# Weights laid out by pairs of units in DRAM: loads and whole-row stores of 6,144 bytes per partition behind attention

## The chip, the cores and the metric

One core of a Trainium2 chip runs the kernel in one launch. The metric is device time in microseconds, the median of several executions; lower is better. Before the change it is 380.92 us (three runs: 380.85, 380.92, 381.82).

## The reference

Sigmoid attention feeds a soft mixture of experts. All tensors are float32.

```python
# attention: B, H, S, D = 8, 12, 448, 64
scores = scale * q @ k.transpose(0, 1, 3, 2) - log(S)
attn_out = (1 / (1 + exp(-scores))) @ v
x = attn_out.transpose(0, 2, 1, 3).reshape(B * S, H * D)      # 3584 x 768
# soft MoE: 8 experts with 4 slots each, w1[e] 768 x 1024, w2[e] 1024 x 768
logits = x @ phi                                              # 3584 x 32
d = softmax(logits, axis=0)
slot_input = (d.T @ x).reshape(8, 4, 768)
for e in range(8):
    slot_out[e] = relu(slot_input[e] @ w1[e]) @ w2[e]
c = softmax(logits, axis=1)
return c @ slot_out.reshape(32, 768)                          # 3584 x 768
```

The weights w1 and w2 are 25.2 MB each and the output is 11.0 MB.

## The kernel before

The program has two parts in a row. **Attention** goes through 168 units `u = (p, c)` (pair of heads, block of 128 keys) in a software pipeline. Per step PE makes the scores of one unit (L188), ScalarE the sigmoid (L196), and PE weighs the values of the unit two steps before (L229). Between these stand the DVE transposes, the logits and the slot sums of the batch before. After the last unit, `last_job` finishes the last batch's logits, softmax and slot inputs, about 278 to 289 us.

**Behind attention** the experts are computed. The weights come in 128 *units* of [128, 768] floats (384 KB, 3,072 bytes per partition): 64 of w1 (expert, half of the rows, quarter of the columns), then 64 of w2 (half of the output columns `hf`, expert, `g`, `y`). `w1_part(e)` takes eight units in two groups of four; `w2_step(n)` takes two units, `y` 0 and 1, of one `(hf, e, g)`. The first column half is computed for all experts (sixteen steps, with the combine softmax turned into lhsT tiles `cts` between them), then the second half (sixteen steps). `spread_sum` sums each half's four partial sums into the tile `sts[hf]`. The output is `cts.T @ sts[hf]` in tiles of 128 tokens by 384 columns, which ScalarE and VectorE copy out of PSUM in turn (L579). `out_half(m, hf)` stores two such blocks of tokens in one half of the columns (runs of 1,536 bytes in DRAM), `out_rows(m)` one block in whole rows (runs of 3,072 bytes). Nine `out_half` for the first half stand among the steps 4 to 12 of the second half; after the second `spread_sum` come ten `out_rows` (blocks 18 to 27) and nine `out_half` for the second half.

All units, `cts` tiles and output tiles go through one ring of 71 slots of [128, 768]: 56 slots `wa` that exist from the start, two in `wpe` (which attention borrows as transposed x), and 13 slots `wb` in the memory that the attention buffers held. 58 units are loaded during attention; the 13 `wb` loads are written behind it, and the other 57 at four places of eight in the `w1_part`s.

Every transfer is issued by SyncE (SP), in the program's order, on one queue. A tile's load waits for the last readers of what lay there before. The transfers take eight semaphores in turn (`DMAHW0` to `DMAHW7`), so each waits for the transfer eight before it, and at most eight are in flight. PE, DVE, ACT and SP take their instructions in the order of the code (`manual_schedule`).

Of the kernel before, what the change touches and what calls it, by code (L numbers as in the profile page):

```python
# [9 lines left out]
F32 = mybir.dt.float32  # L10
F32R = mybir.dt.float32r
# [6 lines left out]
DM, NSLOT, E, SPE, F = 768, 32, 8, 4, 1024  # L18
P = 128
# [8 lines left out]
HALF = DM // 2  # L28
UNIT = 768
N_A = 56  # L30
N_E = 2
N_B = 13
QW = 2 * S
NP = B * NPR
WARM = 5
# [3 lines left out]
BLK = 32  # L39
NEG = -1.0e30  # L40
TR = 3
SLN = TR * 64
FW = (NFC + 1) * NSLOT
ROWS = 128
NG = B * S // ROWS
NH = 18
MANUAL = {mybir.EngineType.PE, mybir.EngineType.SP, mybir.EngineType.DVE, mybir.EngineType.Activation}


@with_exitstack  # L50
def soft_moe_attention(ctx: ExitStack, tc: tile.TileContext, qk, v, vl, phi, w1, w2, cst, out):
    nc = tc.nc
    ctx.enter_context(tc.manual_schedule(engines=MANUAL))

    cpool = ctx.enter_context(tc.tile_pool(name="cpool", bufs=1))
    small = ctx.enter_context(tc.tile_pool(name="small", bufs=1))
    wpa = ctx.enter_context(tc.tile_pool(name="wpa", bufs=1))
# [17 lines left out]

    units = [("w1", e, q, kh) for e in range(E) for kh in range(2) for q in range(4)]
    units += [("w2", hf, e, g, y) for hf in range(2) for e in range(E) for g in range(2) for y in range(2)]
    state = {"next": 0, "ring": 0, "wpb": None}
    utile = {}
    wpe = wpa.tile([P, N_E * UNIT], F32, name="wpe")  # L80

    def ring_tile(dt=F32):
        n = state["ring"] % (N_A + N_E + N_B)
        state["ring"] += 1
        if n < N_A:
            return wpa.tile([P, UNIT], dt, name=f"wa{n}")
        n -= N_A
        if n < N_E:
            return wpe[:, n * UNIT:(n + 1) * UNIT] if dt == F32 else ring_tile(dt)
        return state["wpb"].tile([P, UNIT], dt, name=f"wb{n - N_E}")  # L90

    def load_unit():
        n = state["next"]
        if n >= len(units):
            return
        state["next"] = n + 1
        u = units[n]
        t = ring_tile()[:, :]
        nc.sync.dma_start(t, w1[u[1:]] if u[0] == "w1" else w2[u[1:]])
        utile[u] = t  # L100

    heads = (slice(0, 64), slice(64, 128))
    QSCALE = 1.0 / math.sqrt(D)
# [11 lines left out]
    with ExitStack() as actx:  # L115
# [45 lines left out]
        def load_qk(p):  # L161
            if p < NP:
                t = get("qk", p % 3)
                nc.sync.dma_start(t[:], qk[p])
                qkts[p] = t
# [100 lines left out]
        def logits(lg, b, pairs, js=(3, 2, 1, 0), c0=0, c1=NBK):  # L266
            for hp in pairs:
                for j in js:
                    n = min(c1, nblk(j))
                    nc.tensor.matmul(  # L270
                        lg[32 * j:32 * j + 32, BLK * c0:BLK * n], phi_sb[:, hp, :],
                        blocks(x_of(b * NPR + hp)[:, c0 * P:], j, n - c0),
                        start=(hp == 0), stop=(hp == NPR - 1 and c1 == NBK))
# [149 lines left out]
        for r in range(NP // 2):  # L423
            p = 2 * r
# [3 lines left out]
        for b in range(B):  # L428
            u = b * per_b + LAG
# [4 lines left out]
        for b in range(B - 1):  # L434
            u = (b + 1) * per_b + LAG
# [15 lines left out]
        for i in range(len(seq) + LAG):  # L451
            for f in early.get(i, ()):
                f()
            if i < len(seq):
                u = seq[i]
                score(u)
                if u[1] == NFK:
                    load_qk(u[0] + 3)
                elif u[0] % 2 == 1 and u[1] == NFK - 1:
                    load_qk(u[0] + 3)  # L460
                while state["next"] < min(N_A, (i + 1) * N_A // W_STEPS):
                    load_unit()
                if i == (B - 1) * per_b + LAG + SLOT_AT + 1:
                    for _ in range(N_E):
                        load_unit()
            if i == len(seq) - 1:
                lgt = ps_sc.tile([P, 2, 512], F32, name="sc")
                nc.vector.memset(lgt[64:128, 0, 96:128], NEG)
            if i == len(seq):
                nc.scalar.activation(dmx[0:1, :], atts[seq[-1]][0:1, 0, 0:1], AF.Exp)  # L470
            for f in middle.get(i, ()):
                f()
            if i >= LAG:
                u = seq[i - LAG]
                weigh(u)
                p, c = u
                if i == len(seq):
                    logits(lgt[:, 0, :], B - 1, range(NPR - 1))
                if c == NFK:
                    evac_b(p)  # L480
                    load_vl(p // 2 + 1)
                elif c == NFK - 1:
                    load_v(p + 2)
                    if p == NP - 1:
                        work(B * S)
                        pw = ps_av.tile([P, 512], F32, name="av00")
                        px = [ps_av.tile([P, 512], F32, name="av01")]
                        px += [ps_sc.tile([P, 2, 512], F32, name="sc")[:, 0, :], ps_av.tile([P, 512], F32, name="av10")]
                        turn_pe(px[0], p - 1)
                        continue  # L490
                    evac_a(p)
                    if p % 2 == 1:
                        evac_b(p)
            for f in late.get(i, ()):
                f()
            work(rate.get(i, PACE))
# [12 lines left out]
        turn[name] += 1  # L509
        return ps_av.tile([P, 512], F32, name=f"{name}{turn[name] % 2}")  # L510

    for _ in range(N_B):
        load_unit()

    def w1_part(e, ph=None):
        if ph is None:
            ph = av_tile("av0")
            w1_mm(ph, e, range(TR))
        for _ in range(4):
            load_unit()  # L520
        if e == 0:
            finish(ps_t)
        w1_mm(ph, e, range(TR, NKC))
        for _ in range(4):
            load_unit()
        return ph

    def h_part(e, ph):
# [6 lines left out]
    cts = {}  # L535
# [19 lines left out]
    def combine_turn(b, c4):  # L555
        pt = ps_t.tile([P, 512], F32, name="pt")
        for c in range(NBK):
            n = P if c < 3 else 64
            c0 = c * P if b % 2 == 0 else (c * P + 64) % 448
            nc.tensor.transpose(  # L560
                out=pt[:, c0:c0 + n], in_=c4[0:n, c].rearrange("p a z s -> p (a z s)").bitcast(F32),
                identity=csb[0:n, 0:n])
        at0 = S * b
        while at0 < S * (b + 1):
            i, m = divmod(at0, UNIT)
            w = min(UNIT - m, S * (b + 1) - at0)
            if m == 0:
                cts[i] = ring_tile(F32R)
            nc.scalar.copy(cts[i][:, m:m + w], pt[:, at0 - S * b:at0 - S * b + w])
            at0 += w  # L570

    def ct_of(m):
        i, k = divmod(m * ROWS, UNIT)
        return cts[i][:, k:k + ROWS]

    def out_tile(ov, m, st, hf, n):
        pf = ps_t.tile([P, 512], F32, name="pt") if n % 2 else av_tile("av0")
        nc.tensor.matmul(pf[:, 0:HALF], ct_of(m), st, start=True, stop=True)  # L578
        (nc.scalar.copy, nc.vector.tensor_copy)[n % 2](ov, pf[:, 0:HALF])  # L579

    def out_half(m, hf):
        ov = ring_tile()[:, :].rearrange("p (j c) -> p j c", j=2)
        for j in range(2):
            out_tile(ov[:, j, :], m + j, sts[hf], hf, j)
        nc.sync.dma_start(
            out[m * ROWS:(m + 2) * ROWS, hf * HALF:(hf + 1) * HALF].rearrange("(j p) c -> p j c", p=P), ov)

    def out_rows(m):
        ov = ring_tile()[:, :].rearrange("p (j c) -> p j c", j=2)
        for hf in range(2):  # L590
            out_tile(ov[:, hf, :], m, sts[hf], hf, hf)
        nc.sync.dma_start(out[m * ROWS:(m + 1) * ROWS, :].rearrange("p (j c) -> p j c", j=2), ov)

    sts = []

# [15 lines left out]
    def w2_step(po, hf, n):  # L611
        e, g = divmod(n, 2)
        h = hw[e % 2]
        if g == 0:
            o = NSLOT - SPE
            nc.gpsimd.tensor_copy(
                h[:, o:o + NFC * NSLOT].rearrange("p (f s) -> p f s", f=NFC)[:, :, 0:SPE], hc[:, e])
        for fl in range(4):
            k = (4 * g + fl) * NSLOT + NSLOT - SPE - SPE * e
            ut = utile[("w2", hf, e, g, fl // 2)][:, fl % 2 * HALF:(fl % 2 + 1) * HALF]  # L620
            nc.tensor.matmul(  # L621
                po[32 * fl:32 * fl + 32, 0:HALF], h[:, k:k + NSLOT], ut,
                start=(n == 0), stop=(n == 2 * E - 1))
        load_unit()
        load_unit()

    prev = None
    for e in range(E):
# [17 lines left out]
    for n in range(2 * E):  # L646
        w2_step(po, 1, n)
        if n == 3:
            spread_sum(so)
        if 4 <= n < 4 + NH // 2:  # L650
            out_half(2 * (n - 4), 0)
    spread_sum(gather(po))
    for m in range(NH, NG):
        out_rows(m)
    for m in range(0, NH, 2):
        out_half(m, 1)

# [36 lines left out]
```

## Time and profile before

| What | Value |
|---|---|
| Median of three runs | 380.92 us (380.85 to 381.82) |
| Profiled execution, its own time | 379.96 us |
| Its span, first to last instruction | 378.2 us |
| Mean granted TensorE clock | 0.978 |
| PE / DVE / ACT busy in the span | 355.6 / 252.9 / 224.1 us |
| Bytes moved | 95.29 MB (83.59 MB read from HBM, 11.01 MB written) |
| Load queue | 42,336 packets, 94.62 MB, 72.3% of 16 engines' span |
| Weight loads | 128 of 384 KB |
| Output stores | 28 of 384 KB |

The span is cut by the page into 40 slices; a digit is the busy share in tenths. A share of the DMA engines may be over 1, since packets overlap on an engine. The packets of one transfer are spread over 16 engines; here a packet is one partition's row (or the part of it that is contiguous in DRAM), and each engine adds a packet of 4 bytes for the semaphore. Names such as `wa<-in_w_dram` are destination and source with buffer numbers left out: w1 and w2 both read as `in_w_dram`. L592 is the store of `out_rows`, L585 that of `out_half`, L99 a unit's load, L110 a w1 matmul, L621 a w2 matmul, L329 a matmul that adds the old slot sums in `last_job`.

### The profile page before, as it was taken

Reading aid. Unit: us, or ns where it says so; the run is one execution under the profiler, and the core shown is the slowest. Engines: PE = TensorE matmul, PEld = TensorE weight load, DVE = VectorE, ACT = ScalarE, POOL = GpSimd, SP = SyncE. Lnnn points to the kernel's source line nnn. Section 1 sums busy time; section 2 is a strip of 40 time slices with the busy share of each in tenths; the row PEclk is TensorE's granted clock in tenths of the full one; section 3 lists DMA queues with packets and bytes.
Section 4 is the critical chain, followed back from the end, with each engine's and each line's share of the span. In section 5 each row is a group of like instructions: output and inputs, shape, how many; then the busy total and the mean of one; then the engine's idle time right before and its main releaser. Section 6 shows DMA issues by size and latency. Waiting matters only on the chain.

```text
span 378.2 us, 10668 instructions
## 1 busy us (share of the span) xinstructions
PE 355.6 (94%) x4374; PEld 160.4 (42%) x4374; DVE 252.9 (67%) x681; ACT 224.1 (59%) x311; POOL 5.4 (1%) x25
## 2 busy tenths in 40 slices
PE   8999999999999999999999999999999978989750
PEld 4333444444444444444444444444456643422420
DVE  0148878885989688778859896888746872233560
ACT  4777676766757676767667675767672113422550
POOL 1000000000000000000000000000001000000000
PEclk9999999999999999999999999999999998999895
DMA  7687575766657675756666576433479999999998
GB/s 259 218 257 233 181 252 183 241 224 200 216 175 245 230 216 193 233 199 229 222 207 205 189 267 194 132 123 129 142 232 354 383 400 400 402 400 398 400 407 309
DMA packets 42384, 95.29 MB, mean 252 GB/s; under 512 B 4448, under 2 KB 18528, under 8 KB 42336
## 3 DMA queue, kind: packets, MB, share of 16 engines
q1 hardware_dynamic: 42336, 94.62, 72.3%
q8 instruction: 34, 0.56, 0.6%
q14 instruction: 14, 0.11, 0.1%
HBM read 83.59 MB, written 11.01 MB: 250 GB/s over the span
## 4 chain that ended last, share of the span: by engine, by line
PE 83%; DVE 7%; DMA 4%; ACT 1%; issue 1%; DVEq 0%; ACTq 0%
PE sc L188 34%; PE av L229 33%; PE av L621 5%; PE sc L270 3%; PE sc L323 3%; DMA wpe<-in_w_dram 2%; PE pt L560 2%; DMA out_dram<-wa 1%; DVE tmp L531 1%; DMA qk<-in_qk_dram 1%; DVE tmp L530 1%; PE av L578 1%; PE av L204 1%; DVE wa L579 1%; ACT lt L541 1%
## 5 line engine op out<-in xcount | busy, mean ns | idle before, releaser
L196 ACT ACTIVATE att<-sc,sm 128x896 f32<-128x896 f32 x167 | 168.3, 1008 | 85.1 <-PE sc L188 82.1
L188 PE MATMUL sc<-qk 64*64 64x448 f32 x1336 | 157.2, 542 | 0.5 <-DMA qk<-in_qk_dram 0.5
L229 PE MATMUL av<-att,v 64*64 64x448 f32 x1128 | 131.2, 536 | 0.0
L188 PEld LDWEIGHTS sc<-qk 64*64 64x64 f32 x1336 | 49.8, 134 | 71.5 <-issue 58.8
L254 DVE STREAM_TRANSPOSE wpe<-xy 32x256 f32<-32x256 f32 (+3 forms) x224 | 76.9, 343 | 3.7
L229 PEld LDWEIGHTS av<-att,v 64*64 64x64 f32 x1128 | 42.8, 133 | 63.2 <-issue 61.1
L254 DVE STREAM_TRANSPOSE y<-x 32x288 f32<-32x288 f32 (+1 forms) x128 | 66.5, 520 | 2.0
L236 DVE TENSOR_TENSOR x<-x,av 128x448 f32<-128x448 f32 x24 | 14.9, 621 | 31.5 <-PE av L229 24.5
L229 PE MATMUL av<-att,vl 64*64 64x448 f32 x188 | 22.3, 536 | 0.0
L236 DVE TENSOR_TENSOR xy<-xy,av 128x448 f32<-128x448 f32 x23 | 14.3, 621 | 9.8 <-ACT xy L232 4.5
L110 PE MATMUL av<-wa,jt 128*32 128x256 f32 x336 | 18.5, 380 | 0.1
L110 PEld LDWEIGHTS av<-wa,jt 128*32 128x32 f32 x336 | 10.7, 110 | 7.2 <-DVE jt L385 0.2
L621 PE MATMUL av<-wa,jt 128*32 128x384 f32 x112 | 13.4, 506 | 0.2
L578 PE MATMUL av<-lt,wb 128*128 128x384 f32 x28 | 12.5, 446 | 1.1 <-DVE lt L608 1.0
L232 ACT COPY x<-av 128x448 f32<-128x448 f32 x24 | 12.5, 522 | 0.0
L232 ACT COPY xy<-av 128x448 f32<-128x448 f32 x23 | 12.1, 524 | 0.0
L578 PE MATMUL pt<-lt,wb 128*128 128x384 f32 x28 | 10.5, 376 | 1.6 <-DVE lt L608 1.6
L229 PEld LDWEIGHTS av<-att,vl 64*64 64x64 f32 x188 | 7.3, 133 | 10.7 <-issue 10.7
L342 DVE SCALAR_TENSOR_TENSOR jt<-jt,t,sc 128x192 f32<-128x192 f32 x6 | 2.5, 414 | 13.7 <-PE sc L323 13.7
L579 DVE COPY wa<-pt 128x384 f32<-128x384 f32 x20 | 10.5, 555 | 1.6 <-PE pt L578 1.3
L579 ACT COPY wa<-av 128x384 f32<-128x384 f32 x20 | 9.0, 481 | 4.0 <-PE av L578 3.4
L533 ACT COPY t<-tmp 128x32 f32<-128x32 f32 x8 | 1.7, 218 | 15.9 <-DVE tmp L531 15.9
(132 smaller groups left out, 237.3 us busy)
## 6 DMA issues: line engine op xcount, KB each, us to landing
wa<-in_w_dram SPq DMA_DIRECT2D x112, 384.0 KB, 5.9
qk<-in_qk_dram SPq DMA_DIRECT2D x48, 448.0 KB, 3.8
v<-in_v_dram SPq DMA_DIRECT2D x48, 192.0 KB, 2.8
out_dram<-wa SPq DMA_DIRECT2D x20, 384.0 KB, 5.5
wb<-in_w_dram SPq DMA_DIRECT2D x13, 384.0 KB, 4.7
out_dram<-wb SPq DMA_DIRECT2D x8, 384.0 KB, 7.7
vl<-in_vl_dram SPq DMA_DIRECT2D x24, 64.0 KB, 2.5
wpe<-in_w_dram SPq DMA_DIRECT2D x3, 384.0 KB, 3.6
```

What stands on the lines that cost most here:

```text
L110: nc.tensor.matmul(ph[32 * j:32 * j + 32, 0:256], phi_sb[:, kc, :], utile[("w1", e, j, kc // 3)][:, kc % 3 * 256:(kc % 3 + 1) * 256], star ...
L188: nc.tensor.matmul(sc[h][64 * t:64 * t + 64, 0:S], qkts[pt][r, S + k0:S + k0 + 64], qkts[pt][r, 0:S], start=True, stop=True)
L196: nc.scalar.activation(att[:], tile2[:, :, 0:S], AF.Sigmoid, bias=nbias, scale=QSCALE)
L229: nc.tensor.matmul(o[t][r, 0:S], w, att[row, h, :], start=start, stop=stop)
L232: nc.scalar.copy(x_of(p), avs[p][1][:, 0:S])
L236: nc.vector.tensor_tensor(out=x_of(p), in0=x_of(p), in1=av[0][:, 0:S], op=ALU.add)
L254: nc.vector.transpose(y[32 * g:32 * g + 32, k0:k0 + n, 0:nblk(g), BLK * a:BLK * a + BLK], src)
L270: nc.tensor.matmul(lg[32 * j:32 * j + 32, BLK * c0:BLK * n], phi_sb[:, hp, :], blocks(x_of(b * NPR + hp)[:, c0 * P:], j, n - c0), start=(h ...
L323: nc.tensor.matmul(sls[t][32 * a:32 * a + 32, :], zt[:, c * BLK:(c + 1) * BLK], y_of(t, b)[:, :, c, BLK * a:BLK * a + BLK], start=(c == 0) ...
L578: nc.tensor.matmul(pf[:, 0:HALF], ct_of(m), st, start=True, stop=True)
L579: (nc.scalar.copy, nc.vector.tensor_copy)[n % 2](ov, pf[:, 0:HALF])
L621: nc.tensor.matmul(po[32 * fl:32 * fl + 32, 0:HALF], h[:, k:k + NSLOT], ut, start=(n == 0), stop=(n == 2 * E - 1))
```

## The change

In DRAM, w1 and w2 become one tensor `w` of 64 pairs, [128, 1536] each: two neighbouring units side by side in each partition's row of 6,144 bytes. In SBUF the 56 `wa` slots become 28 tiles of double size, `wpe` is one double slot, and `wb` has six single slots (`N_S`) and three double ones (`N_D`), 70 single slots in all. A `load(1)` takes half of a double slot and half of a pair's rows; that is what attention still does for its 58 units and what fills the six single `wb` slots. A `load(2)` fetches a pair: 3 into `wb`, 28 into `wa` and one into `wpe`. A `cts` tile is now double, too. `out_half` and `out_rows` take half of a double slot; of the ten blocks in whole rows the first two (`NR`) are stored singly and the other eight by `out_rows2`, two blocks at a time: partition p holds the tokens 2p and 2p + 1 of the 256, so that its 6,144 bytes are contiguous in DRAM. For that the matmul's lhsT takes every second column of the `cts` tile (`ct_of(m, 2)`). PE, DVE, ACT and POOL have the same instructions in the same order as before, on other tiles.

```diff
-    def ring_tile(dt=F32):
-        n = state["ring"] % (N_A + N_E + N_B)
...
+    slots = [("wa", n, 2) for n in range(N_A // 2)] + [("wpe", 0, 2)]
+    slots += [("wb", n, 1) for n in range(N_S)] + [("wb", N_S + n, 2) for n in range(N_D)]
+
+    def ring_tile(size=1, dt=F32):
+        while True:
+            pool, n, room = slots[state["ring"] % len(slots)]
+            if state["half"] is not None:
+                t, state["half"] = state["half"], None
+                state["ring"] += 1
+                if size == 1 and dt == F32:
+                    return t[:, UNIT:2 * UNIT]
+                continue
+            if size > room or (pool == "wpe" and dt != F32):
+                state["ring"] += 1
+                continue
...
+            if size < room:
+                state["half"] = t
+            else:
+                state["ring"] += 1
+            return t[:, 0:size * UNIT]
...
-        t = ring_tile()[:, :]
-        nc.sync.dma_start(t, w1[u[1:]] if u[0] == "w1" else w2[u[1:]])
-        utile[u] = t
+        if size == 2 and (state["half"] is not None or slots[state["ring"] % len(slots)][2] == 1):
+            load(1)
+            load(1)
+            return
+        state["next"] = n + size
+        t = ring_tile(size)
+        m = n % 2 * UNIT
+        nc.sync.dma_start(t, w[n // 2][:, m:m + size * UNIT])
+        for k in range(size):
+            utile[units[n + k]] = t[:, k * UNIT:(k + 1) * UNIT]
...
-    for _ in range(N_B):
-        load_unit()
+    for _ in range(N_S // 2 + N_D):
+        load(2)
...
-        for _ in range(4):
-            load_unit()
+        for _ in range(2):
+            load(2)
...
-            if m == 0:
-                cts[i] = ring_tile(F32R)
+            if m == 0 and i % 2 == 0:
+                cts[i] = ring_tile(2, F32R)
+                cts[i + 1] = cts[i][:, UNIT:2 * UNIT]
...
+    def ct_of(m, step):
+        i, k = divmod(m // 2 * 2 * ROWS, UNIT)
+        c = cts[i][:, k:k + 2 * ROWS]
+        if step == 1:
+            return c[:, m % 2 * ROWS:(m % 2 + 1) * ROWS]
+        return c.rearrange("p (r t) -> p t r", t=2)[:, m % 2, :]
...
+    def out_rows2(m):
+        ov = ring_tile(2)
+        for k in range(4):
+            t, hf = divmod(k, 2)
+            out_tile(ov[:, k * HALF:(k + 1) * HALF], m + t, hf, hf, 2)
+        nc.sync.dma_start(out[m * ROWS:(m + 2) * ROWS, :].rearrange("(p t) c -> p (t c)", t=2), ov)
...
-    for m in range(NH, NG):
+    for m in range(NH, NH + NR):
         out_rows(m)
+    for m in range(NH + NR, NG, 2):
+        out_rows2(m)
```

SyncE's queue at the seam between attention and the experts, before: the last eight `wb` slots and the first three `wa` slots (name and slot, an instance number, destination's partitions by elements, and the semaphores that it waits for).

```order
L99 DMA wb5_3554<-in_w1_dram 128x768 [waits DMAHW1_49,PE_49,Activation_49]
L99 DMA wb6_3556<-in_w2_dram 128x768 [waits DVE_49,PE_49]
L99 DMA wb7_3558<-in_w2_dram 128x768 [waits DMAHW3_49]
L99 DMA wb8_3560<-in_w2_dram 128x768 [waits DMAHW4_49,PE_49,Activation_49]
L99 DMA wb9_3562<-in_w2_dram 128x768 [waits DMAHW5_49]
L99 DMA wb10_3564<-in_w2_dram 128x768 [waits DMAHW6_49,PE_49]
L99 DMA wb11_3566<-in_w2_dram 128x768 [waits DMAHW7_49]
L99 DMA wb12_3568<-in_w2_dram 128x768 [waits DVE_49,PE_49,DMAHW0_49,Activation_49,Pool_49]
L99 DMA wa0_3570<-in_w2_dram 128x768 [waits DMAHW1_49]
L99 DMA wa1_3572<-in_w2_dram 128x768 [waits DMAHW2_49]
L99 DMA wa2_3574<-in_w2_dram 128x768 [waits DMAHW3_49]
```

The same place now:

```order
L120 DMA wb5_3526<-in_w_dram 128x768 [waits DMAHW1_49,PE_49,Activation_49]
L120 DMA wb6_3528<-in_w_dram 128x1536 [waits DVE_49,PE_49]
L120 DMA wb7_3530<-in_w_dram 128x1536 [waits DMAHW3_49,PE_49,Activation_49]
L120 DMA wb8_3532<-in_w_dram 128x1536 [waits DMAHW4_49,PE_49]
L120 DMA wa0_3534<-in_w_dram 128x1536 [waits DMAHW5_49,PE_49]
L120 DMA wa1_3536<-in_w_dram 128x1536 [waits DMAHW6_49,PE_49]
```

From `wb6` on one transfer stands for two; the slot `wb12`, which waited for five engines, has no successor, and the pair behind `wb8` waits for PE's last use of the first two w1 units.

SyncE's queue at the end, before: from the last load over the half-row stores (L585) to the whole-row stores (L592).

```order
L99 DMA wa55_3908<-in_w2_dram 128x768 [waits DMAHW0_49,PE_49]
L99 DMA wpe_73<-in_w2_dram 128x768 [waits DMAHW1_49,PE_49]
L585 DMA out_0_dram<-wb5_4158 128x2x384 [waits DMAHW2_49,DVE_49,Activation_49]
...
L585 DMA out_0_dram<-wa0_4258 128x2x384 [waits DMAHW2_49,DVE_49,Activation_49]
L592 DMA out_0_dram<-wa1_4288 128x768 [waits DMAHW3_49,DVE_49,Activation_49]
L592 DMA out_0_dram<-wa2_4296 128x768 [waits DMAHW4_49,DVE_49,Activation_49]
L592 DMA out_0_dram<-wa3_4304 128x768 [waits DMAHW5_49,DVE_49,Activation_49]
```

And now (L611 is `out_half`, L618 `out_rows`, L625 `out_rows2`):

```order
L120 DMA wa27_3816<-in_w_dram 128x1536 [waits DMAHW0_49,PE_49]
L120 DMA wpe_73<-in_w_dram 128x1536 [waits DMAHW1_49,PE_49]
L611 DMA out_0_dram<-wa0_4064 128x2x384 [waits DMAHW2_49,DVE_49,Activation_49]
...
L611 DMA out_0_dram<-wa4_4160 128x2x384 [waits DMAHW2_49,DVE_49,Activation_49]
L618 DMA out_0_dram<-wa4_4160 128x768 [waits DMAHW3_49,DVE_49,Activation_49]
L618 DMA out_0_dram<-wa5_4197 128x768 [waits DMAHW4_49,DVE_49,Activation_49]
L625 DMA out_0_dram<-wa6_4205 128x1536 [waits DMAHW5_49,DVE_49,Activation_49]
```

The order of loads and stores is the same, each store waits for the same semaphore in the turn, and from block 20 on a store holds two blocks of tokens and waits for their four copies.

More of the change, by code (lines that the diff above doesn't have):

```diff
@@ L31 @@
 N_E = 2
-N_B = 13
+N_S = 6
+N_D = 3
 QW = 2 * S
@@ L46, with soft_moe_attention @@
 NH = 18
+NR = 2
 MANUAL = {mybir.EngineType.PE, mybir.EngineType.SP, mybir.EngineType.DVE, mybir.EngineType.Activation}
 @with_exitstack
-def soft_moe_attention(ctx: ExitStack, tc: tile.TileContext, qk, v, vl, phi, w1, w2, cst, out):
+def soft_moe_attention(ctx: ExitStack, tc: tile.TileContext, qk, v, vl, phi, w, cst, out):
     nc = tc.nc
@@ L77, in soft_moe_attention, with load @@
     units += [("w2", hf, e, g, y) for hf in range(2) for e in range(E) for g in range(2) for y in range(2)]
-    state = {"next": 0, "ring": 0, "wpb": None}
+    state = {"next": 0, "ring": 0, "half": None, "wpb": None}
     utile = {}
     wpe = wpa.tile([P, N_E * UNIT], F32, name="wpe")
-    def ring_tile(dt=F32):
-        n = state["ring"] % (N_A + N_E + N_B)
[L84 to L92, printed above, removed]
+    slots = [("wa", n, 2) for n in range(N_A // 2)] + [("wpe", 0, 2)]
[12 more added lines that the diff above has]
+                continue
+            if pool == "wpe":
+                t = wpe
+            else:
+                t = (wpa if pool == "wa" else state["wpb"]).tile([P, room * UNIT], dt, name=f"{pool}{n}")
+            if size < room:
+                state["half"] = t
+            else:
+                state["ring"] += 1
+            return t[:, 0:size * UNIT]
+    def load(size):
         n = state["next"]
@@ L95, in load_unit @@
             return
-        state["next"] = n + 1
-        u = units[n]
-        t = ring_tile()[:, :]
-        nc.sync.dma_start(t, w1[u[1:]] if u[0] == "w1" else w2[u[1:]])
-        utile[u] = t
+        if size == 2 and (state["half"] is not None or slots[state["ring"] % len(slots)][2] == 1):
[8 more added lines that the diff above has]
+            utile[units[n + k]] = t[:, k * UNIT:(k + 1) * UNIT]
     heads = (slice(0, 64), slice(64, 128))
@@ L461, in soft_moe_attention @@
                 while state["next"] < min(N_A, (i + 1) * N_A // W_STEPS):
-                    load_unit()
+                    load(1)
                 if i == (B - 1) * per_b + LAG + SLOT_AT + 1:
                     for _ in range(N_E):
-                        load_unit()
+                        load(1)
             if i == len(seq) - 1:
@@ L510, in av_tile @@
         return ps_av.tile([P, 512], F32, name=f"{name}{turn[name] % 2}")
-    for _ in range(N_B):
-        load_unit()
+    for _ in range(N_S // 2 + N_D):
+        load(2)
     def w1_part(e, ph=None):
@@ L518, in w1_part @@
             w1_mm(ph, e, range(TR))
-        for _ in range(4):
-            load_unit()
+        for _ in range(2):
+            load(2)
         if e == 0:
@@ L523, in w1_part @@
         w1_mm(ph, e, range(TR, NKC))
-        for _ in range(4):
-            load_unit()
+        for _ in range(2):
+            load(2)
         return ph
@@ L566, in combine_turn, with out_tile @@
             w = min(UNIT - m, S * (b + 1) - at0)
-            if m == 0:
-                cts[i] = ring_tile(F32R)
+            if m == 0 and i % 2 == 0:
+                cts[i] = ring_tile(2, F32R)
+                cts[i + 1] = cts[i][:, UNIT:2 * UNIT]
             nc.scalar.copy(cts[i][:, m:m + w], pt[:, at0 - S * b:at0 - S * b + w])
             at0 += w
[L572 to L576, printed above, removed]
+    def ct_of(m, step):
[4 more added lines that the diff above has]
+        return c.rearrange("p (r t) -> p t r", t=2)[:, m % 2, :]
+    def out_tile(ov, m, hf, n, step=1):
         pf = ps_t.tile([P, 512], F32, name="pt") if n % 2 else av_tile("av0")
-        nc.tensor.matmul(pf[:, 0:HALF], ct_of(m), st, start=True, stop=True)
+        nc.tensor.matmul(pf[:, 0:HALF], ct_of(m, step), sts[hf], start=True, stop=True)
         (nc.scalar.copy, nc.vector.tensor_copy)[n % 2](ov, pf[:, 0:HALF])
     def out_half(m, hf):
-        ov = ring_tile()[:, :].rearrange("p (j c) -> p j c", j=2)
+        ov = ring_tile().rearrange("p (j c) -> p j c", j=2)
         for j in range(2):
-            out_tile(ov[:, j, :], m + j, sts[hf], hf, j)
+            out_tile(ov[:, j, :], m + j, hf, j)
         nc.sync.dma_start(
@@ L588, in out_rows @@
     def out_rows(m):
-        ov = ring_tile()[:, :].rearrange("p (j c) -> p j c", j=2)
+        ov = ring_tile().rearrange("p (j c) -> p j c", j=2)
         for hf in range(2):
-            out_tile(ov[:, hf, :], m, sts[hf], hf, hf)
+            out_tile(ov[:, hf, :], m, hf, hf)
         nc.sync.dma_start(out[m * ROWS:(m + 1) * ROWS, :].rearrange("p (j c) -> p j c", j=2), ov)
+    def out_rows2(m):
[4 more added lines that the diff above has]
+        nc.sync.dma_start(out[m * ROWS:(m + 2) * ROWS, :].rearrange("(p t) c -> p (t c)", t=2), ov)
     sts = []
@@ L623, in w2_step @@
                 start=(n == 0), stop=(n == 2 * E - 1))
-        load_unit()
-        load_unit()
+        load(2)
     prev = None
@@ L673 @@
     phi = inputs["moe_phi"].reshape(NKC, P, NSLOT).transpose(1, 0, 2)
-    w1 = inputs["moe_w1"].reshape(E, 2, TR, P, 4, 256).transpose(0, 4, 1, 3, 2, 5).reshape(E, 4, 2, P, UNIT)
-    w2 = inputs["moe_w2"].reshape(E, 4, 2, 2, 2, BLK, 2, HALF).transpose(6, 0, 2, 3, 1, 5, 4, 7)
-    w2 = w2.reshape(2, E, 2, 2, P, UNIT)
+    w1 = inputs["moe_w1"].reshape(E, 2, TR, P, 2, 2, 256).transpose(0, 1, 4, 3, 5, 2, 6).reshape(-1, P, 2 * UNIT)
+    w2 = inputs["moe_w2"].reshape(E, 4, 2, 2, 2, BLK, 2, HALF).transpose(6, 0, 2, 1, 5, 3, 4, 7)
+    w = np.concatenate([w1, w2.reshape(-1, P, 2 * UNIT)])
     cst = np.zeros((P, CW), np.float32)
@@ L680 @@
     cst[:, 128:256] = ar[:, None] % NSLOT == ar[None, :] % NSLOT
-    host = {"qk": qk, "v": vv, "vl": vl, "phi": phi, "w1": w1, "w2": w2, "cst": cst}
+    host = {"qk": qk, "v": vv, "vl": vl, "phi": phi, "w": w, "cst": cst}
     nc = bacc.Bacc("TRN2", target_bir_lowering=False, num_devices=1, dynamic_dma_scratch_size=64)
```

## The prediction, made before the changed kernel had run

> **What bounds the kernel now.** I read the page from the top, then the table of stretches, the queue's packets by stretch, the waits and the timeline of SyncE's queue, and last the end of the chain. The page first:
>
> ```profile
> span 378.2 us, 10668 instructions
> PE 355.6 (94%) x4374; PEld 160.4 (42%) x4374; DVE 252.9 (67%) x681; ACT 224.1 (59%) x311; POOL 5.4 (1%) x25
> ...
> PE   8999999999999999999999999999999978989750
> ...
> DMA  7687575766657675756666576433479999999998
> GB/s 259 218 257 233 181 252 183 241 224 200 216 175 245 230 216 193 233 199 229 222 207 205 189 267 194 132 123 129 142 232 354 383 400 400 402 400 398 400 407 309
> ...
> wa<-in_w_dram SPq DMA_DIRECT2D x112, 384.0 KB, 5.9
> qk<-in_qk_dram SPq DMA_DIRECT2D x48, 448.0 KB, 3.8
> ```
>
> A slice is 9.5 us. Up to slice 30 (about 284 us) PE is full and the transfers are not; from slice 31 on the 16 DMA engines are full to the end. The kernel is two kernels in a row: attention, bound by PE, and everything behind it, bound by the DMA queue. "PE 94%" describes the first. The second in stretches (columns: bounds, length, PE, PEld, DVE, ACT, POOL busy us with counts, clock, DMA share, GB/s):
>
> ```profile
> 278.00:284.00 6.00, 6.00 (x100) 4.13 (x93) 1.50 (x8) 3.75 (x8) 0.00 (x0) 1.00 0.84 262
> 284.00:290.00 6.00, 5.42 (x134) 4.02 (x136) 3.86 (x18) 1.43 (x6) 0.76 (x2) 1.00 0.99 381
> 290.00:296.00 6.00, 6.00 (x120) 3.60 (x116) 4.68 (x17) 1.25 (x5) 0.21 (x1) 1.00 0.96 323
> 310.00:345.00 35.00, 31.01 (x257) 11.63 (x258) 10.67 (x31) 12.17 (x30) 2.72 (x13) 0.95 1.03 401
> 351.00:354.00 3.00, 1.11 (x5) 0.49 (x3) 0.86 (x2) 1.43 (x3) 0.00 (x0) 1.00 1.06 399
> 360.00:365.00 5.00, 4.38 (x18) 2.45 (x17) 5.00 (x10) 4.03 (x10) 0.00 (x0) 1.00 1.03 412
> 369.00:374.00 5.00, 0.00 (x0) 0.00 (x0) 0.00 (x0) 0.00 (x0) 0.00 (x0) 0.50 1.05 389
> ```
>
> 310 to 345 us is loads of 3,072 bytes per partition, 351 to 354 the first half-row stores (runs of 1,536 bytes), 360 to 365 the whole-row stores (3,072), 369 to 374 the last half-row stores, when no engine computes any more. The share is at 1 or above in all four, so the time from about 284 us on is bytes over rate, and only the rate or an idle queue can move the end. (In 369:374 and at the end the producers are done: they never hold the last stores.)
>
> The same four as packets (packets, MB; those under 512 B are the 4-byte semaphore packets, one per transfer and engine; in the first line 3 are of the instruction queues):
>
> ```profile
> DMA packets 4392, 12.03 MB, mean 401 GB/s; under 512 B 487, under 2 KB 487, under 8 KB 4389
> DMA packets 830, 1.20 MB, mean 399 GB/s; under 512 B 51, under 2 KB 830, under 8 KB 830
> DMA packets 752, 2.06 MB, mean 412 GB/s; under 512 B 82, under 2 KB 82, under 8 KB 752
> DMA packets 1348, 1.95 MB, mean 389 GB/s; under 512 B 81, under 2 KB 1348, under 8 KB 1348
> q1 hardware_dynamic: 830, 1.20, 106.4%
> q1 hardware_dynamic: 752, 2.06, 102.9%
> ```
>
> The lines are for 310:340, 351:354, 360:365 and 369:374; the q1 lines for the second and third. One packet, its part of the semaphore packets included, took of an engine: loads 16 x 30 us / 3,902 = 123.0 ns; stores of 1,536 bytes 16 x 3 / 779 = 61.6 ns and 16 x 5 / 1,267 = 63.1 ns; stores of 3,072 bytes 16 x 5 / 670 = 119.4 ns.
>
> **The change, part by part.**
>
> *Pairs of units: the gain.* Behind attention 64 single loads become 32 loads of 6,144 bytes per partition, and 8 whole-row stores become 4. A transfer of 384 KB is 8 packets per engine at 3,072 bytes and 16 at 1,536, each with one semaphore packet. Between the two store sizes the bytes and the semaphore packets are equal and 8 packets differ: 16 x 61.6 - 8 x 119.4 = 30 ns, or 16 x 63.1 - 8 x 119.4 = 54 ns. So a packet costs 3.8 to 6.8 ns beyond its bytes. No row has a 6,144-byte packet or a semaphore packet that blocks; I bound them. A pair saves 8 packets and one semaphore packet per engine. Low end: 8 x 3.8 with the semaphore packet free, 30 ns. The semaphore packet taken as a packet's fixed cost, with the middle of the two stores, 5.3 ns: 9 x 5.3 = 48 ns. Both at 3.8 ns: 34 ns. High end: the recorded packet lengths, 106.4% x 48 us / 779 = 65.6 ns and 102.9% x 80 us / 670 = 122.9 ns (semaphore packets shared out), and 2 x 65.6 - 122.9 = 8.3 ns; 9 x 8.3 = 75 ns. 36 pairs (32 loads, 4 stores) then give 1.1 (30 ns), 1.2 (34), 1.7 (48) and 2.7 us (75). Below that stands zero, if the loads' 123.0 ns (3.6 more than a store's of the same size) are set by the bytes' way out of memory. I take 1.7, since the stores are the nearest rows: same queue, same engines, full.
>
> The Trainium skill ("DMA: Bandwidth & Descriptors", section "iDMA fabric", its table of load streams) has 408.7 GB/s for one stream alone in rows of 4 KiB, which no run here shows. With this trace's 401 at 3,072 bytes, 122.6 ns an engine against 160.4, an estimate by that page is 236 ns at 6,144 bytes, or 416 GB/s, and the sum 2.3 us.
>
> *Loads during attention* stay single; their rows only lie 6,144 bytes apart in DRAM. PE hides them (slices 1 to 30): nothing.
>
> *Waits at the seam.* The three double slots wait for the attention buffers of two former slots each, the next pair for units 0 and 1. SyncE's queue as it was (waits: us in total, times, longest; then the timeline: start, us):
>
> ```profile
> SPq L99 <- DMA wa<-in_w_dram: 28.3, 48, 1.2
> ...
> SPq L592 <- DVE wa L579: 4.4, 4, 3.8
> ...
> SPq L99 <- PE av L329: 2.7, 1, 2.7
> ```
>
> ```profile
> 277.80 11.16 SPq L99 DMA_DIRECT2D wb<-in_w_dram  x11
> ...
> 355.40 8.26 SPq L592 DMA_DIRECT2D out_dram<-wa  x10
> ```
>
> From 277.8 to 289.0 us 11 loads were issued, and from 278 to 290 us 262 x 6 + 381 x 6 = 3.86 MB moved, 9.8 loads: the backlog covered even the 2.7 us wait on L329. A pair waits for the later of two neighbours, whose readers are the same few PE groups, and the slot with the last wait of all (the 13th) is gone. I cost it at nothing, with 0.2 us of doubt either way; with the backlog gone, a wait like L329's would cost its 2.7 us.
>
> *Two loads land together.* Three pieces of the chain that ended last:
>
> ```profile
> 336.08 0.78 PE av L621 x8
> ...
> 342.46 7.68 DMA wpe<-in_w_dram
> 350.18 0.86 PE av L621 x4
> ```
>
> The last load is issued 7.68 us before it lands: eight 0.98 us loads are in flight, and SyncE then waits for the oldest (the 28.3 us in 48 waits above). Behind the last pair PE has 8 matmuls to do instead of 4: at most the 0.78 us of eight more. That path (350.18 to the first whole-row store at 355.40) is covered by the nine half-row stores that are queued behind the loads: 9 x 393,216 B at 399 GB/s = 8.9 us, to about 359.1. Cover 3.7 us; gone, every further us is lost in full. With pairs, sixteen loads' worth is in flight, but each store still waits for the transfer eight before it, so the stores queue behind the last pair as they did.
>
> *Whole-row stores by two tokens.* Such a store waits for four copies instead of two. Ten issues took 8.26 us, behind the queue (0.95 us each); past the first wait of 3.8 us the other three waits on copies add 0.6 us together. Producing is faster than storing, and the first two whole-row stores stay single. Nothing. The matmul's weight operand is read with a step of two elements for these eight blocks: no row shows its price; the cover is the same 3.7 us and it stays on PE, which is idle from 369 on.
>
> *Slots.* 70 in place of 71; combine tiles go to the three double slots, half-row outputs to the old weight slots. Their last readers are the w1 steps and the w2 steps of the first half, long done. All compute instructions stand in the old order. Nothing.
>
> Sum: the profiled execution took 379.96 us (378.2 in the span, 1.8 around it); minus 1.7 gives 378.3. It stands 0.96 us under the median of the three runs, 380.92, so against that median I forecast 379.2 us (-0.45%). A change under 0.3%, 1.14 us, can't be told from none here.
>
> **The rivals.**
>
> *The loads are bound by bytes, not by packets.* For: a load takes 123.0 ns where a store of the same size takes 119.4, and 401 GB/s stands unchanged for 35 us. Against: the stores show a price per packet at about the same rate. Only the four stores gain, 4 x 48 ns = 0.2 us: 380.7, the same.
>
> *The price per packet is at its low end* (3.8 ns, semaphore packets free): 36 x 30 ns = 1.1 us, 379.8, the same by a hair. The Trainium skill speaks for it ("DMA: Bandwidth & Descriptors", "Why small descriptors are slow (HBM only)"): about 3 cycles per packet beside one per 32 bytes, and joining packets is only worth it at 256 bytes and less. By that rule 6,144 bytes take 195 cycles in place of 198, 1.5% of 32 x 1.97 us of loads and 4 x 1.91 of stores, 1.1 us. Its 102 for 99 between the store sizes (3.0%) is just under what the trace shows (2 x 61.6 or 2 x 63.1 for 119.4: 3.2 to 5.7%).
>
> *The rows are cut again:* no packet of a queue of this kernel is over 3,584 bytes (the 448 KB loads). If 6,144 bytes leave as two packets, only 36 semaphore packets go, under 0.3 us: 380.6, the same.
>
> *Slower: longer rows read worse.* The engines' reading places lie twice as far apart, and 290:296 shows that reads of this very kind can fall to 323 GB/s at a share of 0.96 with nothing else different. 32 pairs are 25.2 MB: 62.8 us at 401 GB/s, 64.7 at 389 (the lowest full stretch): +1.9 us, 382.8. It decides below 394 GB/s. Against: 35 us at 401 without a dip.
>
> **How the numbers follow.** Gain by packets 0.57 (own range 378.2 to 379.7, from 2.7 and 1.2 us); bound by bytes 0.16; low end 0.08; cut 0.05; slower 0.14. Faster 0.57, same 0.16 + 0.08 + 0.05 = 0.29, slower 0.14. The range, 378.0 to 381.0, reaches from the high end with the doubt at the seam over all cases of no change, and leaves out the slower case.
>
> **What would show it.** Right: 36 x 128 = 4,608 fewer packets of data and 36 x 16 = 576 fewer semaphore packets, 405 to 417 GB/s in the middle of the loads, over 412 in the double stores, a share at 1 from 284 us to the end, and a span shorter by what the loads and stores saved. Wrong: 401 GB/s again (bytes), under 394 (slower), the old count of packets (cut), a share well under 0.95 between 284 and 290 us (a wait at the seam) or between 355 and 362 us (the cover of the last chain used up).

## The result, and the profile after

| | Median | Runs |
|---|---|---|
| Before | 380.70 us | 22 (378.71 to 382.20) |
| Changed | 378.11 us | 22 (376.79 to 381.10) |

The ratio, which goes by all runs, is 0.9942, 95% interval 0.9926 to 0.9957: 2.2 us less (1.6 to 2.8). (The medians alone lie 2.6 us apart.) Forecast were 1.7 us less. The gain is small, but clear of the scatter.

The profiled execution of the changed kernel took 381.1 us, the slowest of the 22, so its span can't be set against the span of before. It is read in parts. From its page:

```profile
span 379.3 us, 10574 instructions
...
DMA  7577575767566675766675675534479999999997
GB/s 258 167 232 264 178 228 195 263 188 248 169 232 210 214 232 180 235 231 224 193 241 171 235 245 171 164 117 125 143 217 356 400 418 415 416 415 407 366 401 283
DMA packets 37199, 95.28 MB, mean 251 GB/s; under 512 B 3872, under 2 KB 17952, under 8 KB 37152
...
wa<-in_w_dram SPq DMA_DIRECT2D x28, 768.0 KB, 15.2
out_dram<-wa SPq DMA_DIRECT2D x4, 768.0 KB, 7.1
```

The same line of before:

```profile
DMA packets 42384, 95.29 MB, mean 252 GB/s; under 512 B 4448, under 2 KB 18528, under 8 KB 42336
```

There are 42,384 - 37,199 = 5,185 fewer packets (4,608 of data and 576 of semaphores were due, and an instruction queue moved one less; the 6,144-byte rows leave whole), and slices 33 to 36 run at 415 to 418 GB/s where they had 400 to 402. The same bytes move. In stretches (columns as in the prediction):

```profile
284.00:290.00 6.00, 5.51 (x126) 4.36 (x127) 3.71 (x17) 2.36 (x9) 0.41 (x1) 1.00 1.03 392
290.00:296.00 6.00, 5.91 (x118) 3.70 (x114) 4.33 (x18) 0.84 (x3) 0.56 (x2) 1.00 0.89 312
310.00:345.00 35.00, 30.98 (x265) 11.51 (x257) 10.97 (x33) 11.73 (x30) 2.51 (x12) 0.90 1.02 416
354.00:359.00 5.00, 3.36 (x15) 2.27 (x15) 4.06 (x9) 3.26 (x8) 0.00 (x0) 1.00 0.86 328
360.00:365.00 5.00, 4.84 (x20) 2.83 (x20) 5.00 (x11) 4.24 (x11) 0.00 (x0) 1.00 1.01 412
```

310 to 345 us is the gain: 416 for 401 GB/s. The weak stretch at 290 us (312 GB/s) was there before (323). New is the one at 354 to 359 us, share 0.86.

Where did the execution lose it again? The last scores of the last unit, from the chain that ended last, of before and then of after:

```profile
277.69 0.75 PE sc L188 x8
```

```profile
279.57 0.75 PE sc L210 x8
```

Attention ended 1.88 us later. All of that arose in the first 18 us, after which each sigmoid stands exactly 1.88 us later than before. Attention's compute instructions are the same, and in the profiles of the nine other variants (e2 to e10 below) the ninth sigmoid starts at 15.0 to 16.2 us (15.5 before, 17.3 here), also where attention's loads are the changed kernel's. So this delay is this one execution's. From those scores to the span's end it is 100.5 us before and 99.7 after. The trace's semaphore updates, one per engine and transfer, tell why that is not 2.2 us less. Averaged over the 16 engines, the last load landed 68.9 us after the last score matmul had begun, for 71.3 before: 2.3 us less. But the first engine was done with it at 347.2 us and the last at 351.4, a spread of 4.2 us (2.5 before): ten engines were done by 348.2, the other six had fallen back. The last store of the kernel was done on 14 engines by 377.4 us and on the last at 378.3; the late ones end the kernel.

### The profile page after: what moved, and what is told of

The parts are those of the page before. It is cut to its first block, busy times and chain, and to the rows that moved or that the text cites. A ratio compares the mean times of both kernels' runs of the same rounds, so it can differ in the third digit from the quotient of the medians.

```text
span 379.3 us, 10574 instructions
## 1 busy us (share of the span) xinstructions
PE 355.7 (94%) x4374; PEld 159.8 (42%) x4374; DVE 252.5 (67%) x681; ACT 223.8 (59%) x311; POOL 5.4 (1%) x25
## 2 busy tenths in 40 slices
DMA packets 37199, 95.28 MB, mean 251 GB/s; under 512 B 3872, under 2 KB 17952, under 8 KB 37152
## 4 chain that ended last, share of the span: by engine, by line
PE 81%; DVE 7%; DMA 5%; issue 2%; ACT 1%; DVEq 0%; ACTq 0%
PE sc L210 34%; PE av L251 33%; PE av L654 4%; DMA wpe<-in_w_dram 4%; PE sc L292 3%; PE sc L345 3%; PE pt L582 2%; DVE wa L605 1%; DVE tmp L553 1%; DMA qk<-in_qk_dram 1%; DVE tmp L552 1%; PE av L226 1%; ACT lt L563 1%; DVE lt L562 1%; DVE sm L564 1%
## 5 line engine op out<-in xcount | busy, mean ns | idle before, releaser
L605 DVE COPY wa<-pt 128x384 f32<-128x384 f32 x28 | 14.5, 554 | 7.5 <-PE pt L604 5.9
L605 ACT COPY wa<-av 128x384 f32<-128x384 f32 x28 | 12.5, 480 | 11.2 <-PE av L604 10.9
L654 PE MATMUL av<-wa,jt 128*32 128x384 f32 x112 | 11.7, 518 | 0.0
L654 PE MATMUL av<-wa,hw 128*32 128x384 f32 x112 | 11.5, 511 | 0.0
```

What stands on the lines that cost most here:

```text
L654: nc.tensor.matmul(po[32 * fl:32 * fl + 32, 0:HALF], h[:, k:k + NSLOT], ut, start=(n == 0), stop=(n == 2 * E - 1))
```

## The experiments

Two theories. **Packets**: each packet of a DMA engine costs something beyond its bytes, and longer rows mean fewer packets. **Transfers**: fewer, larger transfers pay (fewer issues and semaphores, more bytes in flight). Beside them: what the layout, the stores, the seam and the cover of the last chain do (the cover is the stores that keep the queue busy while PE finishes behind the last load). All ratios are to the kernel before, run beside each variant.

| Run | Edit against the changed kernel | Median us | Ratio (95%) |
|---|---|---|---|
| e1_again | none | 378.12 | 0.9936 (0.9911 to 0.9961) |
| e2_layout | single loads and single stores | 380.24 | 0.9990 (0.9970 to 1.0009) |
| e3_loads | single stores | 378.14 | 0.9944 (0.9922 to 0.9967) |
| e4_stores | single loads | 380.27 | 0.9999 (0.9981 to 1.0017) |
| e5_one_dma | a pair load in runs of 3,072 bytes | 379.86 | 0.9976 (0.9955 to 0.9998) |
| e6_cut1536 | runs of 1,536 bytes | 383.78 | 1.0082 (1.0053 to 1.0111) |
| e7_quads | four units per load | 376.78 | 0.9893 (0.9867 to 0.9919) |
| e8_nh14 | 7 half-row stores per half instead of 9 | 378.93 | 0.9945 (0.9920 to 0.9971) |
| e9_nh6 | 3 half-row stores per half | 383.34 | 1.0078 (1.0048 to 1.0108) |
| e10_octs | eight units per load | 380.38 | 1.0010 (0.9986 to 1.0034) |

**The changed kernel again (e1_again).**

> The changed kernel once more, for a second profile. In the first one attention was 1.88 us later from its first 18 us on, the loads ran at 416 GB/s, and one DMA engine was up to 4.2 us behind the first at a load's end (2.5 us before). If both are chance, the second profile has attention within 0.3 us of before, the stretch from the last sigmoid to the end 2 to 2.6 us shorter than before's 99.6 us, and a median ratio of 0.993 to 0.996. If the pairs themselves delay the start of attention or widen the spread of the engines, both show again: the last sigmoid 1.5 us or more late and a spread over 3.5 us.

The ratio repeats: 0.9936. Its profiled execution took 933.9 us and tells nothing here (the table's median counts it; that of the other five is 377.70). The start of attention was answered by the other profiles above. The spread of the last load's engines was 3.0 us with the layout alone (e2), 3.3 with the stores alone (e4), 3.6 with pair loads (e3), 3.9 in e5, 3.0 in e8, 3.3 in e9 and 2.8 in e7: it does not follow the size of the transfers.

**One part at a time (e2_layout, e3_loads, e4_stores).**

```diff
# e2 and e4: single loads
-        if size == 2 and (state["half"] is not None or slots[state["ring"] % len(slots)][2] == 1):
+        if size == 2:
# e2 and e3: single stores
-NR = 2
+NR = 10
```

> The new layout and ring, but every load is of one unit (3,072-byte rows that lie 6,144 bytes apart) and every whole-row store of one block. Packets theory: the rate of the loads stays at 400 to 403 GB/s, ratio 0.998 to 1.002. Rival, that the layout in DRAM or the slots gain by themselves: over 408 GB/s or a ratio under 0.997. If rows that lie apart read worse: under 396 GB/s and a ratio over 1.003.

> Pair loads, but all ten whole-row stores single. Packets theory: 414 to 418 GB/s in the loads, and nearly all of the gain: 1.9 to 2.5 us, ratio 0.9935 to 0.9955. If the stores carry half of it, 0.997.

> Single loads, and the four double stores. Packets theory: 0.1 to 0.3 us, ratio 0.998 to 1.001, not to be told from none; loads at 400 to 403 GB/s. If the stores carry half of the gain: 0.997.

The packets in 310 to 340 us, of before, e2_layout, e4_stores and e3_loads in four fences:

```profile
DMA packets 4392, 12.03 MB, mean 401 GB/s; under 512 B 487, under 2 KB 487, under 8 KB 4389
```

```profile
DMA packets 4391, 12.02 MB, mean 401 GB/s; under 512 B 488, under 2 KB 488, under 8 KB 4388
```

```profile
DMA packets 4390, 12.03 MB, mean 401 GB/s; under 512 B 486, under 2 KB 486, under 8 KB 4387
```

```profile
DMA packets 2285, 12.50 MB, mean 417 GB/s; under 512 B 254, under 2 KB 254, under 8 KB 2282
```

The layout with everything else single leaves rate and time alone (0.9990), pair loads by themselves bring all of the gain (0.9944 against 0.9942), and double stores bring nothing that can be told (0.9999). In the kernel before, the rows of one unit lie next to one another in DRAM, in e2 they lie 6,144 bytes apart; that both run at 401 GB/s says that what is contiguous beyond one packet does not count.

**Row length or number of transfers (e5_one_dma, e6_cut1536).** Another order of the same numbers in DRAM; the kernel's pair load keeps its one transfer and one semaphore.

```diff
# e5: w[pair][unit, p, 768]; e6: w[pair][half unit, p, 384], with 2 * size runs
-        m = n % 2 * UNIT
-        nc.sync.dma_start(t, w[n // 2][:, m:m + size * UNIT])
+        k0 = n % 2
+        nc.sync.dma_start(
+            t.rearrange("p (u c) -> p u c", u=size), w[n // 2][k0:k0 + size].rearrange("u p c -> p u c"))
```

> A pair of units is still one transfer with one semaphore, but its two units lie apart in DRAM, so that a partition's 6,144 bytes are two runs of 3,072 bytes. It has the changed kernel's number of transfers (32 pair loads) and the old length of the packets in the loads. Packets theory (the row's length pays): loads at 400 to 405 GB/s, gain at most 0.3 us of semaphore packets plus 0.2 of the stores, ratio 0.998 to 1.000. Rival (fewer and larger transfers pay, by issue, semaphores and a deeper queue): 414 to 418 GB/s and a ratio of 0.993 to 0.996.

> The same with runs of 1,536 bytes in all weight loads: a pair is 32 packets per engine instead of 8. Behind attention 32 x 24 + 6 x 8 = 816 more packets per engine than in the changed kernel. Packets theory: at 3.8 to 6.8 ns each (the two store sizes) 3.1 to 5.5 us more than the changed kernel, 381.2 to 383.7 us, ratio to before 1.002 to 1.009, loads at 381 to 395 GB/s. If the loads are bound by bytes out of memory: loads at 400 or more and no loss against before.

Their packets in 310 to 340 us:

```profile
DMA packets 4145, 12.02 MB, mean 401 GB/s; under 512 B 244, under 2 KB 244, under 8 KB 4142
```

```profile
DMA packets 7479, 11.18 MB, mean 373 GB/s; under 512 B 228, under 2 KB 7475, under 8 KB 7475
```

With the number of transfers halved and the rows as before, the loads run at 401 GB/s, exactly as with single loads: the transfers theory falls. The time alone would not settle it: 0.9976 is 0.9 us less with an interval of 0.1 to 1.7, where 0.5 was allowed. The landings, of one profile each, do: averaged over the engines, e5's last load landed 70.6 us after the last score matmul had begun, among the 70.5 to 71.4 of the three profiles with single loads (before, e2, e4), while the four with loads of 6,144-byte rows (changed, e3, e8, e9) have 68.3 to 68.9. The semaphore packets cost nothing that shows: 244 for 487, at the same rate. With rows half as long it is 373 GB/s, slower than the 381 to 395 that were expected, and the time is just over the expected upper end, 383.8 us for 383.7.

**The other way (e7_quads, e10_octs).** Units 70 to 125 lie by fours (by eights) in a tensor of their own, and `wa` becomes 14 slots of four units (7 of eight).

```diff
-        for _ in range(2):
-            load(2)
+        load(4)    # quads: at both places of a w1_part; octs: load(8) at the second only
```

> Four units per load: 14 loads of 12,288 bytes per partition in place of 28 of 6,144, the stores as changed. Packets theory: each saves 8 packets and one semaphore packet per engine, 14 x 9 x 5.3 ns = 0.7 us (0.5 to 1.0) on top of the changed kernel, loads at 423 to 428 GB/s, ratio to before 0.990 to 0.994. Rival (coarser loads cost the last chain its cover, or the engines drift apart further): 0.5 us or more slower than the changed kernel, a spread between the first and the last engine of the last load over 5 us, and a hole in the share behind it.

> Eight units per load: seven loads of 24,576 bytes per partition, which can't start before all of an expert's w1 is read, some 2.5 us later than the first quad. Packets theory alone: 7 x 8 x 9 ns = 0.5 us less than the quads, loads at 429 to 431 GB/s, ratio to before 0.986 to 0.990. With the seam's cover: the backlog of loads at the seam is 2 to 3 units (2 to 3 us); if the first large load comes after it has run dry, all engines idle 1 to 2 us at about 290 us, and the kernel is 0.5 to 1.5 us slower than the quads, ratio 0.991 to 0.995.

Their packets in 310 to 340 us, the changed kernel's first:

```profile
DMA packets 2279, 12.49 MB, mean 416 GB/s; under 512 B 251, under 2 KB 251, under 8 KB 2275
```

```profile
DMA packets 1166, 12.74 MB, mean 425 GB/s; under 512 B 129, under 2 KB 129, under 8 KB 129
```

```profile
DMA packets 591, 12.92 MB, mean 431 GB/s; under 512 B 64, under 2 KB 64, under 8 KB 64
```

Now a price can be read from the loads themselves. One data packet takes of an engine 16 x 30 us over the queue's packets of data (those of the instruction queues, three or four, left out):

| Row | Packets of data in 30 us | ns each | Two of the size above minus this |
|---|---|---|---|
| 1,536 B (e6) | 7,247 | 66.2 | |
| 3,072 B (before) | 3,902 | 123.0 | 9.4 |
| 6,144 B (changed) | 2,024 | 237.2 | 8.8 |
| 12,288 B (e7) | 1,033 | 464.7 | 9.7 |

Each doubling of the row saves about 9 ns, a fixed price per packet from 1,536 to 12,288 bytes. (The octs' window has 524 packets, 916.0 ns each. That would be 13 ns, but with so few packets four more or less in the window change it by 7.) The price is that of a full queue, and not of the whole time: 64 loads of e6 at 16 x 66.2 - 8 x 123.0 = 75 ns are 4.8 us, and e6 lost 3.1 against before (2.0 to 4.2). From 288 to 296 us, where reads were slower than later in every profile, e6 ran at 339 GB/s and the three profiles with single loads at 330 to 384: there the price does not show. Where the rest of the difference comes from is open. The quads are the fastest version that was run: 376.78 us, and their interval (0.9867 to 0.9919) lies below the changed kernel's (0.9926 to 0.9957). Expected were 0.990 to 0.994. Their packets explain 14 x 8 x 9.7 ns = 1.1 us of the 1.9 that lie between the two ratios; the other 0.8 us are not explained, and lie within the quads' own interval (1.0 us either way).

The octs have the best rate and lose it all: 1.0010 lies outside both of the ranges that were expected. Their stretches:

```profile
288.00:290.00 2.00, 1.91 (x43) 1.25 (x39) 1.08 (x5) 0.04 (x1) 0.35 (x1) 1.00 0.96 386
290.00:292.00 2.00, 2.00 (x44) 1.22 (x40) 1.56 (x6) 0.27 (x1) 0.00 (x0) 1.00 0.73 200
292.00:294.00 2.00, 2.00 (x44) 1.22 (x40) 1.49 (x7) 0.53 (x2) 0.21 (x1) 1.00 0.64 258
...
354.00:357.00 3.00, 1.43 (x7) 0.86 (x6) 1.29 (x3) 0.96 (x3) 0.00 (x0) 1.00 0.57 213
357.00:360.00 3.00, 2.94 (x13) 1.80 (x12) 3.00 (x7) 2.58 (x6) 0.00 (x0) 1.00 0.59 231
```

At 290 to 294 us the queue runs dry, as one theory had it: the first large load was issued at 290.67 us, when on most engines the one before it had already landed (on the last engine at 291.41). The second hole, at 354 to 360, is one that only the quads' expectation had named, as a rival: eight units land together at 346.6 us and the last pair at 349.0, and PE then has several steps and output tiles left where the changed kernel had one step, so that the first whole-row store is issued at 357.44, 8.4 us behind the last landing in place of 5.3.

**How much the half-row stores cover (e8_nh14, e9_nh6).**

```diff
-NH = 18
+NH = 14    # e9: 6
```

> The changed kernel with seven half-row stores of each half instead of nine, and six double stores instead of four. Packets theory: two pairs of blocks leave in 8 packets instead of 32 with one semaphore packet less, 2 x (24 x 5.3 + 5) = 0.26 us saved; the cover of the last chain falls from nine half-row stores (8.9 us) to seven (6.9) against the chain's 5.3 us. If the cover holds: 0 to 0.4 us less than the changed kernel, not to be told from none. If it doesn't: 0.5 to 1.5 us more, and a hole in all engines' share at about 355 us.

> The changed kernel with three half-row stores of each half instead of nine, and ten double stores. Each half-row store behind the loads is 0.98 us of cover for the chain from the last load to the first whole-row store. In the run with seven the engines came together (0.2 us apart) behind a hole and the last engine lost about 0.1 us, so nine seem to have 1.9 us to spare, not the 3.7 of the prediction. If so, six fewer lose 5.9 - 1.9 = 4.0 us and save some 0.8 us of packets: 381 to 382 us, ratio to before 1.000 to 1.004. With 3.7 us to spare: 2.2 lost, 0.8 saved, 379.5 us, ratio 0.997. If the stores behind the loads cover nothing: no slower than the changed kernel, 0.992 to 0.995.

With seven the time is the changed kernel's (0.9945), though there is a hole in most engines; with three it is 5 us more than the changed kernel's. The stretch behind the last load, of e8_nh14 and then of e9_nh6:

```profile
350.50:354.00 3.50, 1.93 (x7) 1.46 (x6) 1.67 (x3) 1.21 (x3) 0.00 (x0) 0.80 0.77 289
```

```profile
349.00:351.00 2.00, 1.51 (x8) 0.20 (x8) 0.00 (x0) 0.29 (x1) 0.00 (x0) 0.50 0.41 152
351.00:356.00 5.00, 3.33 (x7) 2.21 (x8) 1.67 (x3) 1.46 (x4) 0.00 (x0) 0.50 0.01 3
```

e9 lost more than the 4 us that were expected (383.3 us for 381 to 382) because its chain was longer, too: TensorE's granted clock was 0.50 there. Pieces of the chain that ended last behind the last load, the changed kernel and then e9_nh6:

```profile
351.42 0.90 PE av L654 x8
...
352.92 0.93 PE av L636 x2
```

```profile
349.09 1.55 PE av L654 x8
...
351.24 1.66 PE av L636 x2
```

The two groups take 1.4 us longer. The runs of e9 say the same: four with a mean clock of 0.965 to 0.968 took 383.2 to 384.6 us, one with 0.975 took 383.0 and one with 0.979 took 381.4. It is not the number of half-row stores that holds the clock up: e5, with all nine, had 0.50 at this place, too.

```profile
351.18 1.17 PE av L655 x8
...
352.95 1.66 PE av L637 x2
```

```profile
357.00:360.00 3.00, 3.00 (x11) 2.54 (x10) 2.60 (x5) 1.97 (x5) 0.00 (x0) 0.50 0.61 238
```

What decides whether the clock falls there is open. The cover by itself: nine half-row stores leave about 1.9 us to spare, the two stores of 0.98 us that e8 did without.

## Why the prediction was right

**Bound and mechanism.** Right. Behind attention time is bytes over rate, and the rate rose by fewer packets. "The loads are bound by bytes" and "cut again" fell to 416 GB/s and to the count of packets; "longer rows read worse" to the same row; the low end (1.1 us) lies outside the measured 1.6 to 2.8. For "cut again" the page of before was misread, too: 42,384 - 42,336 = 48 of its packets were over 8 KB, those of the instruction queues, so that only the load queue had none over 3,584 bytes.

**The size of the gain.** 1.7 us forecast, 2.2 measured: right in sign, small by a quarter, with the terms off in both directions (2.3 us of loads and nothing of stores in place of 1.5 and 0.2). That the median, 378.11 us, lies inside the range is partly luck: it is 0.1 us above the lower end, which the forecast had drawn from its high end and the doubt at the seam. The step that was mis-sized is the price of a packet, taken from the stores at 3.8 to 6.8 ns. In the loads it is 9 ns, so 32 pairs save 8 x 9 x 32 = 2.3 us in place of 1.5. The recorded lengths of the stores' packets, which I used as the high end (8.3 ns), came nearer, but by chance: the loads' own recorded lengths, 102.8% x 480 us / 3,902 = 126.5 ns before and 101.1% x 480 us / 2,024 = 239.8 now, give 13 ns by the same working. The semaphore packet, taken at 5.3 ns, shows no price (e5). And the stores' own price does not go on: in e9, whose ten double stores give a long stretch, 362 to 374 us:

```profile
DMA packets 902, 4.95 MB, mean 413 GB/s; under 512 B 96, under 2 KB 96, under 8 KB 902
```

16 x 12 us / 806 = 238.2 ns for 6,144 bytes, where two of 3,072 bytes took 238.8: the term of 0.2 us for the double stores shows as nothing.

The Trainium skill's 408.7 GB/s in rows of 4 KiB ("DMA: Bandwidth & Descriptors", "iDMA fabric") had led to an estimate of 416 GB/s, and 416 was measured; no run here has rows of 4 KiB. The Trainium skill's rule of about 3 cycles per packet ("DMA: Bandwidth & Descriptors", "Why small descriptors are slow (HBM only)") would have made 3,072 to 6,144 bytes worth 1.5%; here two packets of 123.0 ns became one of 237.2, 3.6%.

**Waits at the seam: nothing.** Right in the main, and closer than it was argued. SyncE's waits of 276 to 300 us on that line of PE, in the changed kernel (2.7 us before):

```profile
SPq L120 <- PE av L351: 5.7, 2, 3.7
```

They doubled. The stretch from 288 to 296 us, of before, of the changed kernel and then of e3_loads, which has the same loads:

```profile
288.00:296.00 8.00, 7.91 (x158) 4.84 (x154) 5.76 (x22) 1.36 (x5) 0.56 (x2) 1.00 0.98 343
```

```profile
288.00:296.00 8.00, 7.91 (x177) 5.06 (x170) 5.31 (x23) 0.84 (x3) 0.56 (x2) 1.00 0.93 326
```

```profile
288.00:296.00 8.00, 7.91 (x154) 4.77 (x146) 6.12 (x24) 1.37 (x5) 0.56 (x2) 1.00 0.99 373
```

In e3 the queue kept its backlog. In the changed kernel's one profile the share fell by 0.05, 0.4 us of the 8, twice the doubt that was allowed. The octs, whose first large load was issued 2.0 us after the quads' (290.67 for 288.72 us), ran dry.

**The last chain's cover.** Right that it holds, wrong in its size: 3.7 us were claimed by counting from a store's issue, but a store's first bytes move only after that (before, the first whole-row store was issued at 355.40 us and done on the first engine at 357.61, and 0.98 us of it are its bytes), and e8 had used the cover up with 2 us less. The chain itself came as said: 5.26 us from the first matmul behind the landing (351.42) to the first whole-row store (356.68), against 5.2 before. The share of 0.86 at 354 to 359 us would have been read as "cover used up"; e8, with a larger hole and no loss, says that engines which are ahead may idle as long as the last one does not.

**What stays open.** Why reads run at only 309 to 388 GB/s from 291 to 296 us in all these profiles, what makes some engines fall back, and where on a packet's way its 9 ns arise: no run separates the engine from the memory.

## What to carry to other kernels

When the DMA engines are full, count packets: a load's contiguous row per partition costs its bytes plus about 9 ns an engine here (rows of 1,536 to 12,288 bytes), so lay weights out so that one row holds what is consumed together, and measure the price on the direction (load or store) that is to change. Merging transfers without lengthening their rows bought no rate. Before making loads larger still, check when the slot is free and what is left to compute when the last one lands: at eight units both ends ran the queue dry.

## What was unexpected in the hardware

- Stores of 3,072 and 6,144 bytes per row ran at 412 and 413 GB/s, while loads went on from 401 over 416 to 425 and 431.
- The 16 engines drift apart by 2.5 to 4.2 us at the last load, and a hole brings them together again (0.2 us apart in e8 behind its hole).
- TensorE's granted clock of 0.50 behind a wait made the short end chain 1.4 us longer in two matmul groups (e9), 1.0 us in e5.
